# V loaded on all partitions, batch 0's q scaled at its cast, loads in another order, the low-rank product in one burst, and new priorities

## The chip, the cores and the metric

The kernel runs on one core of one Trainium2 chip. The metric is device time in microseconds (us) from one launch of the whole kernel; lower is better. The profile names the core's engines PE (TensorE), DVE (VectorE), ACT (ScalarE), POOL (GpSimd) and SP (SyncE, which here only issues DMAs). 16 DMA engines move data; their transfers are issued from SP's queue and from POOL's.

## What is computed

Four batches, each of 8 heads, 768 positions and 64 numbers per head. First a recurrent attention with a decay for each head, then a mixer: a low-rank product along the positions (U is 768x32, V is 32x768), added to x, and a two-layer perceptron along the 512 channels with 2048 hidden units.

```python
# attention, per batch and head
state = gamma * state + outer(k[t], v[t])
y[t] = scale * q[t] @ state
# mixer, x = y with heads side by side: (768, 512) per batch
h = xt @ U @ V                      # xt is x transposed
u = x + h.transpose(0, 2, 1)
ch = np.maximum(u @ w_ch1, 0.0) @ w_ch2
return u + ch
```

The kernel computes the recurrence in blocks: within a block as a masked product of q and k with v, between blocks over a state. The decay is split into a factor gamma^t on the side of q and gamma^-t on the side of k.

## The kernel before

**The planner.** The kernel doesn't issue its instructions in the order of the code. Each step is handed to `Plan.add` with a cost for each engine that may run it (letters PE, A for ACT, D for DVE, P for POOL, S for SP's DMA queue, Q for POOL's), what it reads and writes, a due time `at`, and sometimes an earliest time `hold`. `Plan.schedule` places them one by one: of the steps whose predecessors are placed it takes the one that can start first, and among equals the one with the smaller `at`. A step with several engines goes to the one where it would end first. The resulting order per engine is then written out and is fixed on the chip; the planned times and `hold` only decide that order, while on the chip semaphores decide when an instruction runs. Each engine works through its own list in order. The numbers of the dictionary `X` shift the due times; they have no other use, except `sp`, the distance of two batches, by which the due times of batch b start at `T[b] = 21 + sp*b`.

**Batch 0.** Loads of batch 0 are issued from SP in the order of `ORDER`, which is sorted by the entries `ok0`, `oq0` and so on of `X`: k0, q1, q2, q0, k1, V, v0, k2, v2, v1, k3, q3, U, v3. A digit names a pair of heads. `GATE`, the load before the last that is neither U nor V, is q3: the loads of w1 on POOL's queue wait for it to land, and everything that POOL loads later is in one chain behind them (`load_cast` writes the key "in turn").

`pair(c, ...)` computes one pair of heads: k is scaled with `gv` (`scale`, a product of two inputs), q is cast to bf16 (`cast`, a copy), v is cast; k and q are transposed by PE and evicted to `kT` and `qT`; `score` multiplies them in two pieces of 512 and 256 positions, each followed by a DVE product with a mask into `a`; `states` forms the states between blocks, evicted to `ns`; `query` and `intra` add both parts into one bank; `xout` scales this with `gqn` (gamma^t and the factor 1/8) on DVE into `x`. Then `low0(c)` does the low-rank part for these 128 channels (product with `Ub`, eviction to `pcs`, product with `V4`) and gives the transposed u, which the first layer reads.

Where the planner sees PE idle before 21.5 us of its time, `fill` puts in matmuls that nobody reads (`M<-gT` in the profile).

**V.** V is loaded as 32 rows of 768 numbers on 32 partitions (`Vin`, in the memory of T4), cast by ACT to `V4[:RK]`, copied to four groups of 32 partitions by a matmul with `rep` (four identities side by side, written by four ACT copies), and evicted in two pieces.

**Batches 1 to 3.** k, q and v are loaded in chunks of 128 positions; k and q (in batch 1 only k) are transposed by DMAs that SP issues (`t<-kb`, `t<-qb`), two chunks share one `score` step, then mask, state and `mixes`. `proj` makes the low-rank product with U of a whole batch into the bank Y, in two steps of four and of two blocks of x; `expand` multiplies with V and adds to x. `turn_u` transposes the sums by DMA (`uT<-x`) for the next MLP. `mlp` runs the two layers, the second with seven products instead of eight per block, which needs sums of g (`sums`) and of w2 (`w2_sums`, the tiles T).

## Time and profile before

| | |
|---|---|
| median of 3 runs without profile | 221.57 us (221.29 to 221.57) |
| the profiled execution | 224.22 us, of which the span from first to last instruction is 222.5 us |
| granted PE clock, mean | 1.000 |
| HBM read, written | 27.46 MB, 6.29 MB |
| matmuls of the first layer, M<-uT,w1b | 493, 85.6 us |
| last DVE eviction | 218.68 us, for 0.79 us |

The page of the profile lists the busy time of each engine, then the costliest groups of instructions. A group is a line of the kernel, an engine and an operation with its tiles, written out<-in. Many operations go through helpers and so share a line, L294 for nearly all matmuls; the tile names tell them apart. The timeline gives start, length, engine, line and tiles of runs of instructions; "x6" is six of them and a bracket names what ended the idle time ahead of it. The views by window cut the span into stretches. Times are from the start of the span.

### The profile page before, as it was taken

The page shows a single profiled execution, that of the slowest core. Times are in us where ns is not written, and L with a number is a line of the kernel's source. Part 1 is how long each engine was busy: PE and PEld are TensorE (multiplying, and loading weights), DVE is VectorE, ACT ScalarE, POOL GpSimd, SP SyncE. Part 2 cuts the span into 40 slices and gives each one's busy share as a digit, 9 for nine tenths or more (in the row PEclk, how much of TensorE's full clock was granted, in tenths as well). Part 3 has the DMA queues.
Part 4 walks back from the last instruction along what each step waited for, and adds up shares of the span by engine and source line. Part 5 has one row for each costly group of instructions (what it writes and reads, how often), then busy time and mean ns, then how long its engine had stood idle before and what let it go on. Part 6 is the DMA issues. An engine that isn't in the chain of part 4 may idle for free.

```text
span 222.5 us, 5665 instructions
## 1 busy us (share of the span) xinstructions
PE 211.5 (95%) x2321; PEld 151.8 (68%) x2334; DVE 143.7 (65%) x294; ACT 94.3 (42%) x182; POOL 101.7 (46%) x145
## 2 busy tenths in 40 slices
...
GB/s 164 308 311 124 154 204 210 209 176 213 190 91 239 142 160 195 219 138 150 163 110 195 192 198 292 99 0 3 3 93 144 97 97 0 0 3 0 97 94 94
DMA packets 84618, 30.98 MB, mean 139 GB/s; under 512 B 69328, under 2 KB 82384, under 8 KB 84592
## 3 DMA queue, kind: packets, MB, share of 16 engines
...
q8 instruction: 18, 0.29, 0.6%
...
HBM read 27.46 MB, written 6.29 MB: 152 GB/s over the span
## 4 chain that ended last, share of the span: by engine, by line
PE 68%; DVE 11%; DMA 10%; SPq 5%; issue 2%; ACT 1%; POOL 1%; DVEq 0%; POOLq 0%
PE M L294 58%; PE RR L294 7%; SPq L323 5%; DMA t<-kb 4%; DMA uT<-x 3%; DVE S L291 3%; DMA S<-in_q_dram 3%; DVE x L836 3%; PE Y L294 3%; DVE T L291 2%; DVE w2b L291 1%; DVE gT L291 1%; PE RR L298 1%; POOL t L291 1%; DVE o L1012 1%
## 5 line engine op out<-in xcount | busy, mean ns | idle before, releaser
L294 PE MATMUL M<-uT,w1b 128*128 128x256 bf16 (+1 forms) x493 | 85.6, 324 | 1.7 <-DMA uT<-x 1.0
L902 ACT ACTIVATE gT<-M 128x512 bf16<-128x512 f32 x93 | 55.0, 597 | 39.9 <-PE M L294 39.5
L294 PEld LDWEIGHTS <-w1b 128*128 128x128 bf16 x512 | 47.9, 98 | 31.1 <-DMA uT<-x 1.3
L294 PEld LDWEIGHTS <-gT 128*128 128x128 bf16 x423 | 40.8, 99 | 12.2 <-issue 3.9
L291 POOL TENSOR_TENSOR t<-s,x 128x256 f32<-128x256 f32 x36 | 23.1, 669 | 54.0 <-DVE S L291 38.7
L294 PEld LDWEIGHTS <-S 128*128 128x128 bf16 x288 | 27.6, 98 | 3.9 <-issue 0.5
L291 POOL TENSOR_TENSOR vb<-in,gkn 128x512 bf16<-128x512 f32 x18 | 18.8, 1048 | 24.2 <-DVE S L291 14.0
L287 ACT ACTIVATE s<-M 128x256 f32<-128x256 f32 x12 | 4.6, 383 | 51.4 <-PE M L294 51.4
L294 PE MATMUL M<-w2b,gT 128*128 128x256 bf16 x192 | 26.4, 273 | 0.0
L291 DVE TENSOR_TENSOR S<-gT 128x512 bf16<-128x512 bf16 x24 | 10.9, 456 | 23.4 <-ACT gT L902 23.4
L294 PE MATMUL M<-w2b,S 128*128 128x256 bf16 x192 | 26.1, 273 | 0.0
L294 PE MATMUL M<-T,gT 128*128 128x256 bf16 x192 | 25.2, 273 | 0.3 <-DVE r L1012 0.2
L759 DVE TENSOR_TENSOR a<-RR,mask 128x1024 bf16<-128x1024 f32 x18 | 21.6, 1218 | 2.3 <-PE RR L294 2.1
L332 POOL DMA_DIRECT2D kb<-in_k_dram x18 | 16.6, 920 | 4.6 <-PE M L294 4.0
L1012 DVE TENSOR_TENSOR r<-M,t 128x256 f32<-128x256 f32 x24 | 10.0, 422 | 11.5 <-POOL t L291 10.7
L836 DVE TENSOR_TENSOR x<-RR,x 128x512 bf16<-128x512 f32 x24 | 15.4, 682 | 2.7 <-PE RR L294 2.7
L1054 POOL DMA_DIRECT2D out_dram<-o x18 | 10.4, 581 | 11.3 <-DVE o L1012 11.3
L798 DVE TENSOR_TENSOR x<-RR,gqn 128x512 bf16<-128x512 f32 x18 | 12.3, 686 | 3.7 <-PE RR L294 3.7
L294 PEld LDWEIGHTS <-t 64*128 64x128 bf16 (+2 forms) x304 | 10.4, 98 | 6.1 <-issue 2.6
L1012 DVE TENSOR_TENSOR o<-M,r 128x256 f32<-128x256 f32 x24 | 10.1, 421 | 5.8 <-PE M L294 5.8
L287 ACT ACTIVATE ns<-Y 64x256 bf16<-64x256 f32 x28 | 10.5, 376 | 7.3 <-PE Y L294 6.1
L294 PE MATMUL M<-T,S 128*128 128x256 bf16 x96 | 12.6, 273 | 0.3 <-DVE T L291 0.3
...
## 6 DMA issues: line engine op xcount, KB each, us to landing
...
```

Of the source, the lines that this page charges most:

```text
L287: return nc.scalar.activation(dst, src, AF.Copy)
L291: return (nc.vector if e == "D" else nc.gpsimd).tensor_tensor(dst, a, b, op=op)
L294: nc.tensor.matmul(out_, lhsT, rhs, start=start, stop=stop, skip_group_check=True)
L298: nc.tensor.transpose(out_, in_, ident)
L323: ins = nc.sync.dma_start(out=dst, in_=src)
L332: ins = nc.gpsimd.dma_start(out=dst, in_=src)
L759: add({"D": cD(2 * DM)}, lambda e, a=a, lo=lo: nc.vector.tensor_tensor(a[:, :2 * DM].rearrange("p (n t) -> p n t", t=P), RR[lo // 2].rearr ...
L798: add({"D": cD(DM)}, lambda e, n=n, bank=bank: nc.vector.tensor_tensor(v8(xs[b % 2][:, n]), v8(bank), g8(gqn, n), op=ALU.mult), [bk, "gqn" ...
L836: add({"D": cD(512)}, lambda e, xj=xj, src=src: nc.vector.tensor_tensor(xj, src, xj, op=ALU.add), [f"RR{c}" for c in cc] + kk, kk + [("u", ...
L902: nc.scalar.activation(dst, src, AF.Relu)
L1012: add({"D": cD(HD)}, lambda e: nc.vector.tensor_tensor(dst, bankof(bank)[:, :HD], src, op=op), [bank] + rd, wr, at - X["dv"])
L1054: lambda e: (nc.sync if last else nc.gpsimd).dma_start(out=dst, in_=src), rd, [("out", b, at)], at,
```

## The change

Six things change.

1. V is loaded as 128 partitions of 192 numbers (partition 4r+z has quarter z of row r). A cast of 192 columns makes `Vb`; four selection matrices `sel`, made by four DVE comparisons of an iota `at4` on POOL with the partition number, each pick one quarter and copy it to four groups of 32 rows, in four matmuls of 192 columns; one eviction of 768 columns follows. `rep` is gone.
2. In batch 0 q is no longer copied to bf16 but multiplied with `gq` (gamma^t and 1/8, in the layout of q) by DVE or POOL, as the planner chooses; `xout` becomes a plain copy from the bank, on ACT or DVE. `gqn` is still used in batches 1 to 3 and made later. The k scaling of pairs 2 and 3 may go to DVE too.
3. Loads of batch 0: q1, k0, q0, q2, V, k1, v0, k2, v1, k3, v2, q3, U, v3. The gate is q3 as before.
4. `proj` is one step of six blocks.
5. The filler counts have other factors, and the first filler step is held to 2.3 us.
6. All other numbers of `X` are new, new ones are added that shift steps of `pair` and `low0`, and two planned costs of DMAs differ (packet lengths, the tail of a transpose).

```diff
 ALU = mybir.AluOpType
 
 
-X = dict(ok0=-5.67, oq0=1.84, ok1=1.9, oq1=-0.6, ov0=3.14, ok2=5.26, oq2=1.45,
-         ok3=15.06, oV=2.44, oq3=17.18, ov1=13.19, ov2=6.5, ov3=18.48, oU=18.06, lq=17.99,
-         tr=0.24, tq=10.94, ex=-12.82, rl=-2.43, su=-4.19, e0=10.6, h0=4.72, w2=13.24,
-         sp=49.61, s1=21.14, pl=7.44, dv=11.91, cs=-1.39, cm=-10.37, cz=-3.97, l01=18.56,
-         l11=8.4, lh1=7.26, lv1=-0.63, c01=16.51, c11=6.16, pr1=46.27, tu1=48.21, td1=7.82,
-         cd1=2.53, vd1=-4.64, l02=-11.92, l12=14.31, lh2=-6.66, lv2=-24.37, c02=8.2, c12=10.8,
-         pr2=24.03, tu2=46.43, td2=-2.58, cd2=-1.75, vd2=-9.06, l03=-9.78, l13=11.82,
-         lh3=-18.87, lv3=-4.29, c03=-2.28, c13=9.08, pr3=21.72, tu3=34.68, td3=5.36,
-         cd3=-10.86, vd3=2.96)
+X = dict(ok0=1, oq0=2, ok1=5, oq1=0, ov0=6, ok2=7, oq2=3, ok3=9, oV=4, oq3=11, ov1=8,
+         ov2=10, ov3=13, oU=12, lq=-45.23, tr=-14.91, tq=-38.01, ex=7.83, rl=-14.32, su=18.99,
+         e0=6.44, h0=5.37, w2=-3.71, sp=46.89, s1=48.11, pl=32.09, dv=17.7, cs=-53.8,
+         cm=-25.93, cz=13.57, l01=-35.68, l11=36.86, lh1=11.83, lv1=2.13, c01=39.94, c11=-6.13,
+         pr1=23.15, tu1=51.34, td1=66.28, cd1=-25.8, vd1=-20.06, l02=-6.29, l12=10.42, lh2=0.5,
+         lv2=-29.02, c02=-23.8, c12=1.28, pr2=10.89, tu2=25.84, td2=1.3, cd2=10.29, vd2=31.92,
+         l03=5.32, l13=13.9, lh3=-10.93, lv3=-39.66, c03=-25.14, c13=2.38, pr3=30.22, tu3=18.6,
+         td3=-54.16, cd3=-30.22, vd3=-22.97, ka0=42.09, ka1=-5.31, ka2=-11.97, ka3=6.36,
+         qa0=27.76, qa1=-35.86, qa2=-44.9, qa3=-88.92, va0=6.17, va1=7.23, va2=-25.67,
+         va3=38.79, sa0=22.39, sa1=-10.15, sa2=11.68, sa3=16.82, st0=0.17, st1=15.58,
+         st2=-6.01, st3=24.5, mx0=-8.83, mx1=27.0, mx2=-20.81, mx3=-39.06, lo0=-6.27,
+         lo1=34.38, lo2=1.06, lo3=-1.13)
 
 
 def Xb(n, b):
...
             if op.eng == "PE":
                 gap = op.start - last - 0.12
                 if fill and op.start < until and gap > 0.1:
-                    fill(int(gap * (1.25 if last < 13 else 1.0) / (0.44 if last < 4 else 0.218)))
+                    fill(int(gap / (0.36 if last < 4 else 0.2)))
                 last = op.free
             ins = op.fn(op.eng)
             if op.eng == "D" and "D" in op.lock:
...
     gv = sb.tile([P, NC, 2, NB, 2], fp32, name="gv")
     gqn = sb.tile([P, NCK, H], fp32, name="gqn")
     gkn = sb.tile([P, NCK, H], fp32, name="gkn")
+    gq = sb.tile([P, H, NCK], fp32, name="gq")
     ns = sb.tile([P, 12, P], bf16, name="ns")
 
     def ring(n, shape, dtype, name):
...
             lambda e: both(e, dst, src, g, ALU.mult), rd, wr, at, lock="DP")
 
     def packet(size):
-        return {128: 0.014, 256: 0.0195, 512: 0.0265}.get(size, 0.0055 + size / 27000)
+        return {128: 0.0135, 256: 0.0195, 512: 0.027, 1536: 0.065}.get(
+            size, 0.0055 + size / 27000)
 
     def load(dst, src, nd, size, wr, at, hold=0.0, rd=(), tail=1.0, held=None):
         def f(e):
...
     add({"D": 0.22}, lambda e: nc.vector.tensor_scalar(
         mask, jmat, srange[:, 0:1], None, op0=ALU.is_ge), rd=["jmat"], wr=["mask"],
         at=late + 6, hold=late + 6)
+    ramp(gq, [NCK, H, 1], [[0, H], [1, NCK]], NCK,
+         lgt[:, :, None].to_broadcast([P, H, NCK]), 1.0, "gq", late)
     for t, sign, key in ((gqn, 1.0, "gqn"), (gkn, -1.0, "gkn")):
         ramp(t, [NCK, H, 1], [[P, NCK], [0, H]], 1,
-             lgt[:, None, :].to_broadcast([P, NCK, H]), sign, key,
-             late if sign > 0 else 25.0)
+             lgt[:, None, :].to_broadcast([P, NCK, H]), sign, key, 25.0)
 
 
     def xk(b, nn, cc):
...
                  [(key, y) for y in ((0, 1) if g is None else (g,))] + ["turn"], at + 0.01 * z, hold,
                  tail=0.8 if (nm, c, z) == ("k", 0, 0) else 1.2, held=held)
 
+    KE, QE = ("D", "D", "PD", "PD"), ("PD", "PD", "PD", "PD")
+
     def pair(c, at, atq, atv, between):
 
         last = c == NC - 1
+        at, atq, atv = at + Xb("ka", c), atq + Xb("qa", c), atv + Xb("va", c)
+        ats, mat = atq + Xb("sa", c), max(atv + 2.6, atq + 4.5) + Xb("mx", c)
         (kin, kk), (qin, qk), (vin, vk) = (gets.pop((nm, 0, c)) for nm in "kqv")
         (kb, kbk), (qb, qbk), (vb, vbk), (kT, kTk), (qT, qTk) = (
             (t[:, :S], key) for t, key in (r() for r in (
...
             scale(blocks_of(kb, g), heads(kin, g),
                   gk[:, g[0]:g[0] + len(g)].to_broadcast([P, len(g), 6, D]), w,
                   [(kk, i) for i in g] + ["gv"], [(kbk, i) for i in g],
-                  at + 0.1 * g[0], eng="D" if c < 2 else "P")
-        cast(blocks_of(qb, (0, 1)), heads(qin, (0, 1)), S, both2(qk), both2(qbk), atq,
-             eng="PA")
+                  at + 0.1 * g[0], eng=KE[c])
+        scale(blocks_of(qb, (0, 1)), heads(qin, (0, 1)),
+              gq[:, 2 * c:2 * c + 2, :, None].to_broadcast([P, 2, NCK, D]), S,
+              both2(qk) + ["gq"], both2(qbk), atq, eng=QE[c])
         if last:
             vv = [t[:, :S].rearrange("p (i n x) -> p i n x", i=2, n=NB) for t in (vb, vin)]
             cast(vv[0][:, :, :2], vv[1][:, :, :2], 512, [(vk, 0)], [(vbk, 0)], atv,
...
         for bs in ((0, 1), (2,)):
             w = 256 * len(bs)
             add({"PE": 0.115 * len(bs) + (0.06 if last and bs[0] else 0)}, score(bs),
-                [kTk] + both2(qTk), keys, atq + 2.2 + 0.5 * bs[0], ("ss", "ss"))
+                [kTk] + both2(qTk), keys, ats + 2.2 + 0.5 * bs[0], ("ss", "ss"))
             held = []
 
             def masks(e, bs=bs, w=w, held=held):
...
                     .to_broadcast([P, 2, len(bs), 256]), op=ALU.mult))
 
             add({"D": cD(2 * w)}, masks, keys + ["mask2"], blocks(ak, bs),
-                atq + 2.4 + 0.5 * bs[0])
+                ats + 2.4 + 0.5 * bs[0])
 
             def copy_cross(e, held=held):
                 after(copy(e, cross[:64], RR[0][:64, :, 256:]), held[0])
 
             if last and bs[0]:
                 add({"A": cA(512)}, copy_cross, keys + blocks(ak, bs) + ["cross0"], ["cross", ("T", 0)],
-                    atq + 3.6)
+                    ats + 3.6)
 
         def state(parts, start):
             def f(e):
...
 
         whole = [(1, 0, P), (2, 0, P), (3, 0, P), (4, 0, P), (3, 1, P), (4, 1, P)]
         half = [(0, 0, 64), (2, 1, 64)] + ([] if last else [(4, 2, 64)])
-        sat = atv + (0.6 if last else 1.5)
+        sat = atv + (0.6 if last else 1.5) + Xb("st", c)
         vks = [(vbk, 0)] if last else both2(vbk)
 
         def states(e):
...
                        vb[:, ds(384 * i + P * 2 + D * j, D)], start=False)
 
         xv = xs[0].rearrange("p (b cc) f -> p cc b f", cc=2)
-        gx = gqn.rearrange("p (b cc) h -> p cc b h", cc=2)
-        mat = max(atv + 2.6, atq + 4.5)
 
         def both_(*fs):
             def f(e):
...
 
         def xout(cc, bs, bank, keys, at):
             n = len(bs)
-            add({"D": cD(P * n)}, lambda e: nc.vector.tensor_tensor(
-                xv[:, cc, ds(bs[0], n), ts(c, P)].rearrange("p b (i d) -> p b i d", d=D),
-                bank.rearrange("p (b i d) -> p b i d", i=2, d=D),
-                gx[:, cc, ds(bs[0], n), ds(2 * c, 2), None].to_broadcast([P, n, 2, D]),
-                op=ALU.mult), keys + ["gqn"], xk(0, [2 * b0 + cc for b0 in bs], [c]), at)
+            evac(xv[:, cc, ds(bs[0], n), ts(c, P)], bank.rearrange("p (b f) -> p b f", b=n),
+                 P * n, keys, xk(0, [2 * b0 + cc for b0 in bs], [c]), at)
 
         if not last:
             add({"PE": 0.28 + 0.36 + 0.093}, both_(query(range(1, NCK)), intra(range(NB))),
...
             for i, (src, sk) in enumerate(turned):
                 add({"S": 1.26}, lambda e, src=src, i=i, tr=tr: nc.sync.dma_start(
                     out=tr[:, i], in_=src[:, :DM], transpose=True), zz(sk),
-                    [(trk, i)], at - Xb("td", b), dma=(512, 0.0188, 0.7, 1.2))
+                    [(trk, i)], at - Xb("td", b), dma=(512, 0.0188, 0.7, 1.5))
             qT, qTk = [tr[:, 1, c] for c in ALLC], [(trk, 1)]
             if b == 1:
                 qT = [uTs[1][:, c, ts(n, P)] for c in ALLC]
...
                         mm(Y[ds(RK * c, RK), :P], Ub[:, j], xs[b % 2][:, j, ts(c, P)],
                            start=(j == 0), stop=(j == NCK - 1))
             return g
-        add({"PE": 0.25}, f(range(4)), xk(b, range(4), ALLC) + ["Ub"], ["Y"], at,
-            ("cn", "cn"), slack=sl)
-        add({"PE": 0.13}, f(range(4, 6)), xk(b, range(4, 6), ALLC) + ["Ub"], ["Y"],
-            at + 0.1, ("cn", "cn"), slack=sl)
+        add({"PE": 0.38}, f(ALLN), xk(b, ALLN, ALLC) + ["Ub"], ["Y"], at, ("cn", "cn"),
+            slack=sl)
         evac(pcs, Y[:, :P], P, ["Y"], ["pcs"], at + 0.3)
 
     def expand(b, j0, nj, at):
...
     def turn_u(b, j, at):
         add({"S": 1.26}, lambda e: nc.sync.dma_start(
             out=uTs[b % 2][:, :, ts(j, P)], in_=xs[b % 2][:, j], transpose=True),
-            [("u", b % 2, j, z) for z in range(2)], [("uT", b % 2, j)], at, dma=(512, 0.0188, 0.7, 1.2))
+            [("u", b % 2, j, z) for z in range(2)], [("uT", b % 2, j)], at,
+            dma=(512, 0.0188, 0.7, 1.5))
 
 
     W1 = [(0, 256), (256, 256), (512, 512), (1024, 512), (1536, 512)]
...
 
 
     zero = gT[:, 0, :512]
-    add({"PE": 0.43}, lambda e: mm(M[0], zero[:, :P], zero), rd=[("g", 0, 0)],
-        wr=["M0"], at=-10, mode=F)
+    add({"PE": 0.6}, lambda e: mm(M[0], zero[:, :P], zero), rd=[("g", 0, 0)],
+        wr=["M0"], at=-10, mode=F, hold=2.3)
 
     U0, FILL = 21.0, 21.5
     NAMES = [f"{n}{c}" for n in "kqv" for c in ALLC] + ["V", "U"]
...
     gate, GATE = [], [n for n in ORDER if n[0] not in "UV"][-2]
     Vin, Uin = T4.bitcast(fp32), T2.bitcast(fp32)
     Vin, Uin = (t_.rearrange("p a b -> p (a b)") for t_ in (Vin, Uin))
+    Vin = Vin[:, :S // 4]
     Uin = Uin[:, :NCK * RK].rearrange("p (j r) -> p j r", j=NCK)
     stage = [new_in() for _ in range(8)]
     for z, big in enumerate((S1, S2)):
...
         land[n] = t + 1.2
         at = -10 + land[n]
         if n == "V":
-            load(Vin[:RK, :S], moe_V, RK, 3072, ["Vin", "turn"], at, tail=1.2)
+            load(Vin, moe_V.rearrange("r (z x) -> (r z) x", z=4), P, S,
+                 ["Vin", "turn"], at, tail=1.2)
         elif n == "U":
             load(Uin, moe_U.rearrange("(j p) r -> p j r", p=P), S, 128,
                  ["Uin", "turn"], at, tail=1.2)
         else:
             load_pair(n[0], int(n[1]), at, stage.pop(0), held=gate if n == GATE else None)
 
-    rep = sb.tile([P, P], bf16, name="rep")
-
-    def repl(e):
+    QV = S // 4
+    sel = T3[:, ds(4, 2)].rearrange("p a (b m) -> p (a b) m", m=P)
+    Vb, at4 = T3[:, 6, :QV], tmp["r5"][:, :P]
+
+    def choose(e):
         for z in range(4):
-            copy(e, rep[:RK, ts(z, RK)], ident[:RK, :RK])
-    add({"A": 0.8}, repl, ["ident"], ["rep"], at=-2)
-
-    cast(V4[:RK], Vin[:RK, :S], S, ["Vin"], ["V1"], land["V"], eng="AP")
+            ins = nc.vector.tensor_scalar(sel[:, z], at4, srange[:, 0:1], float(-z),
+                                          op0=ALU.subtract, op1=ALU.is_equal)
+        return ins
+    add({"P": 0.3}, lambda e: iota(at4, [[0, 4], [4, RK]], 0), wr=["at4"], at=-2.5)
+    add({"D": 0.9}, choose, ["at4", "jmat"], ["sel"], at=4.5)
+    add({"A": cA(QV, True), "D": cD(QV)}, lambda e: copy(e, Vb, Vin), ["Vin"], ["Vb"],
+        land["V"])
 
     def rep_v(e):
-        mm(RR[1][:, 0], rep[:RK], V4[:RK, :512])
-        mm(RR[1][:, 1, :256], rep[:RK], V4[:RK, 512:])
-    add({"PE": 0.4}, rep_v, ["rep", "V1"], ["RR2", "RR3"], at=land["V"] + 1,
-        mode=("rn", "rn"))
-    evac(V4[:, :512], RR[1][:, 0], 512, ["RR2"], ["V1", "V4a"], land["V"] + 1.1, eng="AD")
-    evac(V4[:, 512:], RR[1][:, 1, :256], 256, ["RR3", "V4a"], ["V1", "V4"],
-         land["V"] + 1.2, eng="AD")
+        for z in range(4):
+            mm(RR[1][:, z // 2, ts(z % 2, QV)], sel[:, z], Vb)
+    add({"PE": 0.36}, rep_v, ["sel", "Vb"], ["RR2", "RR3"], at=land["V"] + 1, mode=F)
+    evac(V4.rearrange("p (z x) -> p z x", z=2), RR[1][:, :, :2 * QV], S, ["RR2"], ["V4"],
+         land["V"] + 1.1, eng="AD")
+
     def low0(c):
-        at = land[f"v{c}"] + (4.0 if c < 3 else 2.0)
+        at = land[f"v{c}"] + (4.0 if c < 3 else 2.0) + Xb("lo", c)
         x = xs[0]
         last = c == NC - 1
         r = ds(RK * c, RK)
```

## The prediction

> **What bounds the kernel now.** I read the page first, then busy time by stage, then the waits of the tensor engine, then the timeline of the stages that the change touches.
>
> ```profile
> span 222.5 us, 5665 instructions
> ...
> PE 211.5 (95%) x2321; PEld 151.8 (68%) x2334; DVE 143.7 (65%) x294; ACT 94.3 (42%) x182; POOL 101.7 (46%) x145
> ```
>
> From the page: PE is busy nearly throughout. That is no proof that nothing can be gained, because filler matmuls count as busy. So I cut the span at points where the timeline changes character.
>
> ```profile
> 1.33:21.40 20.07, 18.54 (x252) 10.21 (x255) 10.61 (x27) 11.61 (x23) 10.21 (x19) 1.00 0.89 247
> 21.40:32.00 10.60, 10.36 (x242) 7.32 (x242) 7.76 (x15) 6.04 (x14) 8.06 (x12) 1.00 1.15 170
> 32.00:46.00 14.00, 13.84 (x114) 6.95 (x113) 8.04 (x13) 9.94 (x17) 8.33 (x10) 1.00 1.38 208
> 46.00:58.00 12.00, 11.44 (x126) 8.72 (x126) 11.62 (x28) 7.71 (x16) 3.84 (x5) 1.00 1.45 194
> 58.00:72.00 14.00, 12.06 (x146) 10.13 (x144) 13.25 (x26) 3.38 (x9) 8.59 (x12) 1.00 1.33 168
> ...
> 122.00:140.00 18.00, 16.96 (x167) 12.55 (x167) 11.74 (x24) 4.76 (x11) 10.47 (x15) 1.00 1.75 216
> ...
> 200.00:222.50 22.50, 18.83 (x172) 16.49 (x169) 8.90 (x22) 1.84 (x5) 5.76 (x9) 1.00 0.19 71
> ```
>
> Columns: stretch, length, then busy time of PE, weight loads, DVE, ACT, POOL, the granted clock, the DMA share, GB/s. Three things are to be seen. From 21.4 us on PE has little air: what is left is 0.16 us in the third row, 0.56 in the fourth, 1.94 in the fifth, 1.04 in the sixth, 3.70 us together, and 3.67 us in the last row, which is the tail of last evictions and stores that nothing here touches. From 46 to 72 us DVE is busy 24.87 of 26 us, so there DVE limits beside PE. Before 21.4 us PE waits for the loads and fills in.
>
> ```profile
> PE M L294 <- DMA uT<-x: 1.0, 1, 1.0
> PE RR L294 <- DMA t<-kb: 0.9, 1, 0.9
> PE RR L294 <- DVE a L759: 0.6, 1, 0.6
> ```
>
> These are PE's three longest waits after 21 us: two transposing DMAs that landed late and a mask product. The start itself is paced by loads:
>
> ```profile
> 14.00:16.00 2.00, 1.69 (x42) 1.27 (x36) 2.00 (x3) 1.92 (x5) 1.44 (x1) 1.00 1.04 308
> 16.00:18.00 2.00, 1.91 (x66) 1.33 (x65) 1.48 (x2) 1.10 (x2) 1.64 (x2) 1.00 1.14 322
> 18.00:20.00 2.00, 1.58 (x45) 1.03 (x40) 1.83 (x4) 0.48 (x1) 0.87 (x2) 1.00 0.32 90
> 20.00:22.00 2.00, 1.47 (x51) 1.22 (x52) 1.04 (x2) 1.95 (x5) 2.00 (x3) 1.00 0.25 39
> ```
>
> Loads run at 308 to 322 GB/s up to 18 us and then fall off; the weights of the first MLP are held behind load q3. The bytes ahead of q3 are the same before and after the change (everything but U and v3), so I take this gate as fixed.
>
> **The change, part by part.** The profiled run's span is 222.5 us, and 1.7 us more lie around it (224.22 us in all). The median without a profile is 221.57. I work out differences in the span and put them on the median.
>
> *Load order and the scaled q.* The rows of the first pairs:
>
> ```profile
> 6.66 0.84 ACT L287 ACTIVATE qb<-in 128x768 bf16<-128x768 f32 x1 [2.21 <-DMA in<-in_q_dram]
> ...
> 8.23 0.82 POOL L288 CAST qb<-in 128x768 bf16<-128x768 f32 x1 [2.53 <-DMA in<-in_q_dram]
> ...
> 9.48 0.84 ACT L287 ACTIVATE qb<-in 128x768 bf16<-128x768 f32 x1 [1.29 <-DMA in<-in_q_dram]
> ...
> 10.38 0.51 PE L298 MATMUL M<-ident,qb 128*128 128x128 bf16 x6 [0.18 <-ACT qb L287]
> ...
> 10.73 1.24 PE L294 MATMUL M<-gT 128*128 128x512 bf16 x5
> 10.90 0.96 DVE L291 TENSOR_TENSOR kb<-in,gv 128x768 bf16<-128x768 f32 x1 [5.68 <-DMA in<-in_k_dram]
> 10.93 0.81 ACT L287 ACTIVATE t<-M 128x768 bf16<-128x768 bf16 x1 [0.60 <-PE M L298]
> ...
> 12.69 0.42 PE L294 MATMUL RR<-t,t 64*64 64x128 bf16 x16
> ...
> 13.96 1.47 POOL L291 TENSOR_TENSOR kb<-in,gv 128x768 bf16<-128x768 f32 x1 [0.46 <-DMA in<-in_k_dram]
> ```
>
> Before, q0 is the last of three q loads and is cast at 9.48; the first score runs at 12.69. After, the order is q1, k0, q0, q2, V, k1, v0, k2, v1, k3, v2, q3, U, v3, so q0 takes the arrival that q2 had, 8.23. k0 comes one load later, with q1 by 6.66, and its scaling, transposes and eviction (0.96+0.51+0.81) end by 9.0, still in time. q0's scaling costs 0.96 on DVE, by the k row of the same shape, where DVE is idle 5.68 us ahead of 10.90; its eviction takes 0.81. With 0.51 for its transposes that is 8.23+0.96+0.51+0.81 = 10.5 for the first score, about 2 us sooner. v1 ahead of v2 brings pair 1's states forward in the same sense.
>
> What does this pay? The stretch from 21.4 to 32 is 10.36 of 10.60 full of real PE work, so only work that moves ahead of it counts. Room for that: PE's idle time in the four rows from 14 to 22 us (0.31+0.09+0.42+0.53 = 1.35), and the 1.24 us of filler at 10.73. So the gain lies between nothing and 2.6 us. Against it stands q3:
>
> ```profile
> 19.52 0.84 ACT L287 ACTIVATE qb<-S 128x768 bf16<-128x768 f32 x1 [2.39 <-DMA S<-in_q_dram]
> ```
>
> q3 is the last q, its cast waits for the landing, and the score waits for it. Its scaling takes 0.96 on DVE or 1.47 on POOL instead of 0.84, so 0.12 to 0.63 us are lost there. Choosing POOL for the other three is covered by its waits for loads. The rows give POOL 1.47 against DVE 0.96, a factor of 1.5. [...]
>
> The scaling of the outputs goes from a DVE product to a plain copy on ACT or DVE:
>
> ```profile
> L642 DVE TENSOR_TENSOR x<-RR,gqn x8: 415/548/558, 18.1 to 29.5; 128x384 bf16<-128x384 f32 x6, 128x256 bf16<-128x256 f32 x2
> ```
>
> That is 6 x 0.55 + 2 x 0.42 = 4.1 us of DVE between 18 and 30, of which some goes to ACT, against about 3.8 us of q products, most of them before 15 us. DVE alternates masks and outputs in this stretch, so this helps to realise the earlier start more than it adds to it. I take for the start PE's idle 1.35 less 0.12 for q3: **-1.2 us**, bounds +0.6 and -2.6. The fillers are counted anew, 5 per us of planned gap instead of 5.7 up to 13 us; I price that inside these bounds.
>
> *V on 128 partitions.*
>
> ```profile
> 1.21 0.29 DVE L365 TENSOR_SCALAR ident<-jmat,srange 128x128 bf16<-128x128 f32 x1
> ...
> 11.63 0.83 ACT L287 ACTIVATE V<-T 32x768 bf16<-32x768 f32 x1
> ...
> 13.63 0.87 ACT L287 ACTIVATE V<-RR 128x512 bf16<-128x512 f32 x2 [0.36 <-PE RR L294]
> ...
> 20.26 0.35 ACT L287 ACTIVATE Ub<-T 128x192 bf16<-128x192 f32 x1
> ```
>
> ACT's cast of 768 columns becomes one of 192, 0.35 by ACT's 128x192 copy of U; two evictions of 0.87 become one of 0.81. Four selections on DVE (4 x 0.29 = 1.2) fall into DVE's idle time before 10.9. PE moves 768 columns as before. V4 is used only by the low-rank step, after U. So some 0.5 us of ACT go, at a place where ACT is not last: **0**, bounds +0.3 (the selections delay a k scaling by one of them) and -0.5. The load keeps its bytes.
>
> *Low-rank product in one burst.*
>
> ```profile
> 81.88 0.45 PE Y L294 x24
> ...
> 113.84 0.34 PE Y L294 x16
> ...
> 119.56 0.23 PE Y L294 x8
> ```
>
> Batch 1 already runs all 24 matmuls together (first row); batch 2 runs them in two pieces, 0.57 in sum. The eviction waits for both anyway, so nothing is late by joining them. **-0.1 us**, bounds 0 and -0.2.
>
> *Priorities.* The planner takes, on each engine, what can start first, and only ties go by priority. But MLP products and attention chunks are tied all the time, so nearly every due time counts. Batch length 49.61 becomes 46.89; the last sums of batch 2 (blocks 4 and 5 of x) were due at 70.6+24.0+4 = 98.6 and are due at 67.9+10.9+4 = 82.8, ahead of the products of the MLP before. The rows:
>
> ```profile
> 122.65 8.24 SPq L864 DMA_TRANSPOSE uT<-x  x6
> ...
> 134.20 0.39 PE L294 MATMUL M<-uT,w1b 128*128 128x512 bf16 x1 [0.99 <-DMA uT<-x]
> ```
>
> Batch 2's last transposes go out only by 130.9 and land at 134.2, while PE has run out of MLP work. Earlier sums put them out earlier, and this 1.0 us should go; that is the step I trust most. Queue order on POOL's DMAs is fixed by the program (one chain), so its loads don't move, whatever their new due times. For the 1.94 us from 58 to 72 I expect little: the late t<-kb depends on loads that don't move. Bounds: -3.7 (all idle time of the stages goes), and on the other side new waits of the size 0.9, one for each of the nine chunk scores but the one that has it, +7.2. I take **-0.9 us**, the one row less a tenth for the engine's change of work.
>
> Sum: -1.2 + 0 - 0.1 - 0.9 = -2.2 us; 221.57 - 2.2 = 219.4 us.
>
> **Rivals.**
>
> *Given back at DVE and w2 (near no change).*
>
> ```profile
> 55.29 0.88 POOL L332 DMA_DIRECT2D in<-in_v_dram  x1 [0.76 <-DMA w2b<-in_moe_w_ch_dram]
> ...
> 58.64 0.43 DVE L291 TENSOR_TENSOR T<-w2b,T 128x512 bf16<-128x512 bf16 x1
> 58.66 0.38 PE L294 MATMUL M<-T,S 128*128 128x256 bf16 x2 [0.29 <-DVE T L291]
> ```
>
> The last quarter of w2 lands about 55.2, fixed by the gate; its four sums (0.43 each, 1.7 together) make 57 the earliest end, and the product that needs them ran to 58.66. With DVE 24.87 of 26 us busy a start that is 1.2 us sooner only waits longer there. Then only the burst and a part of the uT wait remain: 221.57 - 0.1 - 0.2 = 221.3. For it: the DVE row. Against: 6 us of DVE idle from 32 to 46, and the due times of the w2 sums move ahead.
>
> *All of it works.* Start -2.6, burst -0.2, and the first three waits (1.0+0.9+0.6 = 2.5): -5.3, so 216.3. For it: the reasons above hold at once. Against: t<-kb hangs on loads that don't move.
>
> *New waits in PE's order (slower).* One mechanism: PE runs in order; chunk scores are put ahead of MLP products as soon as the plan believes their transposed k landed. The landings of the t transposes spread widely:
>
> ```profile
> DMA to landing us min/median/max: 3.0/5.4/10.6
> ```
>
> Each score that reaches PE's head too early costs some 0.9, as t<-kb did, with MLP products queued behind it. Two such waits eat the 1.3 us of start and burst; from there on the kernel is slower. With three and the uT wait as it was: -1.3 + 2.7 = +1.4, 223.0. For it: attention due times of batch 2 (first chunks 8.2 to -23.8) moved far ahead, and DMA shares of 1.3 to 1.75 from 32 to 140 make landings late. Against: only one such wait among nine scores now.
>
> **How the numbers follow.** Forecast 0.53, given back 0.15, all works 0.10, new waits 0.22. The forecast's own range goes from the start at its largest gain (219.4-1.4 = 218.0) to the start at its loss (219.4+1.8 = 221.2). The range reaches to the price of new waits, 223.0, and down to 217.0; a part of all works and the worse half of new waits lie outside, some 0.2. A measurement here can tell about 0.2%, 0.44 us. Faster: 0.50 of the forecast's share, 0.05 of given back, 0.10: 0.65. Same: 0.02 and 0.09: 0.11. Slower: 0.01, 0.01 and 0.22: 0.24.
>
> **What the profile after would show.** First score near 10.5 instead of 12.69; the first MLP matmuls of batch 0 in a row by about 30.8 instead of 32.04; the outputs' scaling gone from DVE; no uT<-x among PE's long waits and the six transposes out before 125; t<-kb still there once. It would be wrong if the first score is sooner and MLP still starts at 32 (PE order, not arrivals), if the idle time from 46 to 72 grows by what the start gained, or if PE shows three or more waits on t transposes.

## The result, and the profile after

The changed kernel took 224.83 us (median of 6 executions, 223.24 to 226.43) against 221.60 us of the kernel before on the same chip (6, 221.29 to 223.08): ratio **1.0122, 95% interval 1.0085 to 1.0159**, so about 2.7 us slower. A second set gave 225.26 against 222.46 us, ratio 1.0100 (1.0058 to 1.0141). The forecast of 219.4 us and its range up to 223.0 both missed; the sign is that of the rival "new waits in PE's order". A ratio leaves out executions over 1.5% longer than their kernel's fastest, for some kernels below nearly half of them, so a median over all executions, given where it tells more, can be up to 0.5% worse than the ratio says.

The page of the changed kernel, and its busy time by stage (columns as before):

```profile
span 221.6 us, 5665 instructions
...
PE 209.8 (95%) x2325; PEld 151.4 (68%) x2325; DVE 144.7 (65%) x300; ACT 95.2 (43%) x182; POOL 98.8 (45%) x143
```

```profile
21.40:32.00 10.60, 10.60 (x147) 6.22 (x147) 3.92 (x10) 7.45 (x18) 5.92 (x9) 1.00 1.20 184
...
58.00:72.00 14.00, 13.91 (x176) 12.21 (x175) 13.05 (x28) 2.92 (x8) 8.97 (x13) 1.00 0.88 155
...
97.00:122.00 25.00, 24.85 (x322) 21.16 (x320) 21.09 (x41) 9.48 (x21) 15.79 (x20) 1.00 1.41 153
122.00:140.00 18.00, 14.61 (x132) 9.69 (x129) 9.41 (x17) 4.56 (x9) 8.09 (x12) 1.00 1.59 173
140.00:160.00 20.00, 18.99 (x190) 13.76 (x191) 13.52 (x26) 10.91 (x19) 3.13 (x3) 1.00 0.40 60
```

The share of PE is the same 95%, and says nothing. The stages do: in this execution PE is idle from 122 to 160 us for 3.39 + 1.01 = 4.40 us. The waits of PE after 21 us in this execution name the cause:

```profile
PE RR L298 <- DMA t<-qb: 3.9, 2, 2.3
PE RR L302 <- DMA x<-in_q_dram: 1.2, 1, 1.2
PE Y L298 <- POOL vb L295: 0.5, 1, 0.5
PE RR L298 <- DVE a L765: 0.3, 1, 0.3
```

The waits for uT<-x and t<-kb are gone, that for the mask is halved. Two waits of a score for a transposed q have come, and they are 1.6 and 2.3 us long instead of 0.9.

To know what the start gained, the profile that the prediction read is not enough: that execution took 224.22 us, 2.6 us more than the median of 221.60. A second profile of the kernel before is of an execution of 221.89 us, and is the one compared with from here on.

> The kernel before once more, for the size of the start's gain. The profile of it that the prediction read had q3 cast at 19.52 us and the first layer of batch 0 in a row from 32.04. If the change's start is 3 to 4 us sooner because of the change, this profile shows q3 at 18.5 to 20 and the row at 31 to 33. If that profile was merely late (loads that came late in that one execution), q3 is at 17 to 18 here and the row at 28 to 30, and the start's true gain is 1 us or less. Time: 221.3 to 222.9 us.

Measured: 221.89 us, span 220.1; q3 is cast at 18.03, between the two ranges, and the row starts at 31.02, in the first. So that profile was late by 1.0 to 1.5 us, and the start still gains more than 1 us. Its timeline around the start, PE, ACT and POOL:

```profile
12.35 0.42 PE L294 MATMUL RR<-t,t 64*64 64x128 bf16 x16
...
18.03 0.84 ACT L287 ACTIVATE qb<-S 128x768 bf16<-128x768 f32 x1 [1.34 <-DMA S<-in_q_dram]
...
18.30 1.68 POOL L332 DMA_DIRECT2D w1b<-in_moe_w_ch_dram  x2 [0.65 <-DMA S<-in_q_dram]
...
31.02 4.28 PE L294 MATMUL M<-uT,w1b 128*128 128x512 bf16 x19
```

The changed kernel at the same places:

```profile
9.80 0.42 PE L298 MATMUL RR<-t,t 64*64 64x128 bf16 x16
...
17.00 0.96 DVE L295 TENSOR_TENSOR qb<-S,gq 128x768 bf16<-128x768 f32 x1 [0.34 <-DMA S<-in_q_dram]
...
17.27 3.93 POOL L337 DMA_DIRECT2D w1b<-in_moe_w_ch_dram  x5 [0.43 <-DMA S<-in_q_dram]
...
27.69 5.57 PE L298 MATMUL M<-uT,w1b 128*128 128x512 bf16 x25
```

The first score is 2.55 us sooner, q3 and the gate 1.0 us, the first layer in a row 3.33 us. In a second profile of the changed kernel they are at 10.49, 17.54, 17.82 and 28.52, so the gains are 1.9, 0.5, 0.5 and 2.5 us there. The prediction's profile, with the row at 32.04, would have put another 1.0 us on this.

Where the gain went is seen best at one point in each batch: the end of the last matmul of its first layer, read from PE's timeline (us).

| kernel, execution | batch 0 | batch 1 | batch 2 | batch 3 | span |
|---|---|---|---|---|---|
| before, 221.89 | 56.57 | 108.30 | 158.35 | 198.01 | 220.1 |
| changed, 223.40 | 53.78 | 107.03 | 158.93 | 199.58 | 221.6 |
| changed, second profile, 224.63 | 54.13 | 110.08 | 160.14 | 200.79 | 222.9 |
| lh2 4 us earlier (below), 220.04 | 53.94 | 107.07 | 155.57 | 196.21 | 218.3 |

The start is 2.4 to 2.8 us ahead at the end of batch 0's first layer. By the end of batch 2's it is gone: between the two points the changed kernel needs 105.2 and 106.0 us, the kernel before 101.8.

The points don't stand behind quite the same work. At the first, the kernel before has done one score of batch 1 that the changed kernel does just behind it (0.56 us), so the like-for-like gain of the start is 1.9 to 2.2 us. At the third, the kernel before has done most of batch 3's low-rank product, which the changed kernel does later (0.8 us of PE). Its rows, and the changed kernel's:

```profile
154.22 0.52 PE L294 MATMUL Y<-x,Ub 128*32 128x128 bf16 x24
...
157.30 1.05 PE L294 MATMUL M<-uT,w1b 128*128 128x256 bf16 x8
```

```profile
152.66 6.28 PE L298 MATMUL M<-uT,w1b 128*128 128x256 bf16 x56
...
162.36 0.52 PE L298 MATMUL Y<-x,Ub 128*32 128x128 bf16 x24
```

With both put right, the changed kernel loses 3.6 to 4.5 us between the points. The 0.8 us show again in the stretch up to batch 3's point, which takes 40.65 us against 39.66, and as long in the remedied kernel.

### The profile page after: what moved, and what is told of

Read it like the earlier page. It is cut to its first block, busy times and chain, and to the rows that moved or that the text cites. A ratio compares the mean times of both kernels' runs of the same rounds, so it can differ in the third digit from the quotient of the medians.

```text
span 221.6 us, 5665 instructions
## 1 busy us (share of the span) xinstructions
PE 209.8 (95%) x2325; PEld 151.4 (68%) x2325; DVE 144.7 (65%) x300; ACT 95.2 (43%) x182; POOL 98.8 (45%) x143
## 4 chain that ended last, share of the span: by engine, by line
PE 57%; DMA 19%; DVE 10%; SPq 7%; POOL 3%; issue 2%; ACT 1%; POOLq 0%; DVEq 0%
PE M L298 48%; DMA t<-qb 10%; DMA x<-in_q_dram 7%; PE RR L298 6%; SPq L328 5%; DMA S<-in_q_dram 3%; DVE S L295 3%; SPq L742 2%; DVE T L295 2%; POOL w1b L337 2%; PE Y L298 2%; DVE x L840 2%; DVE a L765 1%; POOL vb L295 1%; DVE gT L295 1%
## 5 line engine op out<-in xcount | busy, mean ns | idle before, releaser
L298 PE MATMUL M<-uT,w1b 128*128 128x256 bf16 (+1 forms) x504 | 87.3, 325 | 0.0
L298 PEld LDWEIGHTS <-gT 128*128 128x128 bf16 x412 | 39.7, 99 | 10.6 <-issue 3.7
L298 PE MATMUL M<-w2b,S 128*128 128x256 bf16 x192 | 26.6, 273 | 0.0
L291 ACT ACTIVATE ns<-Y 64x256 bf16<-64x256 f32 x26 | 9.8, 376 | 17.9 <-PE Y L298 13.6
## 6 DMA issues: line engine op xcount, KB each, us to landing
w1b<-in_moe_w_ch_dram POOLq DMA_DIRECT2D x3, 512.0 KB, 10.5
```

The lines of the kernel that those rows point to most:

```text
L291: return nc.scalar.activation(dst, src, AF.Copy)
L298: nc.tensor.matmul(out_, lhsT, rhs, start=start, stop=stop, skip_group_check=True)
```

## Why PE waits

A score of a pair of blocks needs four transposes (kb and qb of each block), issued from SP's queue. Rows of the changed kernel, SP and PE, and below them the time from issue to landing of the transposes issued at 124.14 and at 131.38 us, from the view of the DMAs narrowed to each:

```profile
99.60 0.94 PE L298 MATMUL RR<-t 64*128 64x128 bf16 x16
...
105.87 0.62 PE L298 MATMUL RR<-t 64*128 64x128 bf16 x16
...
114.55 7.97 SPq L868 DMA_TRANSPOSE uT<-x  x6
122.62 1.42 SPq L742 DMA_TRANSPOSE t<-kb  x1
124.14 1.41 SPq L742 DMA_TRANSPOSE t<-qb  x1
...
131.90 0.40 PE L298 MATMUL RR<-t 64*128 64x128 bf16 x8 [1.56 <-DMA t<-qb]
...
140.49 0.40 PE L298 MATMUL RR<-t 64*128 64x128 bf16 x8 [2.31 <-DMA t<-qb]
```

```profile
t<-qb SPq DMA_TRANSPOSE x1, 7.7
...
t<-qb SPq DMA_TRANSPOSE x1, 9.0
```

124.14 + 7.7 = 131.84 and 131.38 + 9.0 = 140.38: the two waits end 0.06 and 0.11 us after these landings. A score that isn't split and waits for nothing takes 0.62; the one at 99.60 took 0.94, since its last q landed at 95.03 + 5.0 = 100.03, after it had begun. So a small part of a wait hides in a long duration. The same places in the kernel before:

```profile
101.19 0.62 PE L294 MATMUL RR<-t 64*128 64x128 bf16 x16
...
112.89 2.10 SPq L736 DMA_TRANSPOSE t<-kb  x1
...
120.51 8.62 SPq L864 DMA_TRANSPOSE uT<-x  x6
...
128.60 0.62 PE L294 MATMUL RR<-t 64*128 64x128 bf16 x16
```

There batch 3's second block is transposed at 112.89, ahead of uT<-x; in the changed kernel at 122.62, behind it. All margins, worked out in this way (start of the score less the landing of its last transpose, us; below zero PE waits):

| | batch 2, 2nd pair | batch 2, 3rd pair | batch 3, 1st pair | batch 3, 2nd pair |
|---|---|---|---|---|
| before | +1.1 | +4.6 | +9.0 | +3.6 |
| changed | -0.4 | +0.6 | -1.9 | -2.6 |
| changed, second profile | -1.6 | -1.5 | -0.3 | -2.1 |
| lh2 4 us earlier | +0.1 | +2.6 | +1.0 | -0.3 |
| lh2 8 us earlier | +3.1 | +6.1 | +0.5 | -0.7 |

In the first execution the landings of batch 2 are no later than before (100.0 against 100.1, 105.3 against 106.5 us), and the scores come 1.6 and 5.2 us sooner. In batch 3 it is the other way round: the scores hardly moved (129.94 against 128.60, 137.78 against 139.16), and the landings come 12.2 and 4.8 us later. The changed kernel has next to no margin left: the first execution loses it mainly in batch 3, the second in both. The waits of PE in its second profile are in part put down to something else:

```profile
101.73 0.40 PE L298 MATMUL RR<-t 64*128 64x128 bf16 x8 [1.36 <-DVE a L765]
...
109.14 0.40 PE L298 MATMUL RR<-t 64*128 64x128 bf16 x8 [1.29 <-DVE a L765]
...
141.53 0.40 PE L298 MATMUL RR<-t 64*128 64x128 bf16 x8 [1.92 <-DMA t<-qb]
```

But the last transposes for these scores, issued at 97.00 and 103.19, took (view of the DMAs, narrowed to each)

```profile
t<-qb SPq DMA_TRANSPOSE x1, 4.6
...
t<-qb SPq DMA_TRANSPOSE x1, 5.8
```

so they landed at 101.60 and 108.99, 0.13 and 0.15 us ahead of the matmuls. The mask that ended in between belongs to the first half of the same score, and the second half, which writes another bank and stands ahead of that mask in the plan, has no need of it. I count all three as late transposes: 4.6 us in this execution, 3.9 in the first and the 0.3 that hides in its long score.

## The experiments

Two theories at first. **DUE**: the new priorities put scores where transposes have not landed, and the start is sound. Rival **START**: one of the three edits of the start loses time.

**Priorities put back, new start kept.** All entries of `X` but those of batch 0's start (`ok0` to `oU`, `ka0` to `lo3`) and the planned tail of a transpose are as before:

```diff
-                    [(trk, i)], at - Xb("td", b), dma=(512, 0.0188, 0.7, 1.5))
+                    [(trk, i)], at - Xb("td", b), dma=(512, 0.0188, 0.7, 1.2))
```

> The changed kernel with every due time that does not belong to batch 0's start (all of X but the load order and the new entries for pair and low0), and the planned tail of a transposing DMA, put back to the values of before. The profile of the changed kernel had the first long row of MLP matmuls at 27.69 us instead of 32.04. Theory DUE (the new due times of batches 1 to 3 make PE wait for transposed q and k, and so give back what the start gained): the row still starts at 27 to 28.5, and the time is 217 to 219.5 us. Rival STREAM (PE has caught up with the loads of batches 2 and 3, and any due times wait for them): the row starts at 27 to 28.5 and the time is 221.5 to 225.

Measured: 223.16 us, in STREAM's range and above DUE's; ratio 1.001 (0.9973 to 1.0047). So the loss goes with the priorities, but the old ones don't turn the start into time either. That kernel's longest waits of PE are 2.1 us for uT<-x and, in three parts, 1.1 for DVE's o.

**The counterpart**: the kernel before's start (copied q, old order, V on 32 partitions) under the other new priorities.

> The kernel before with only the due times outside batch 0's start, and the planned tail of a transpose, taken from the change; load order, q, V, fillers and proj as before. MLP row at about 32. DUE: the new due times lose 4 us or more on their own, so 224 to 228 us. STREAM: the start is as late as before, PE is not ahead of the loads, so 220 to 222.5 us.

Measured: 226.73 us, in DUE's range; ratio 1.0167 (1.0102 to 1.0233). The priorities alone cost about what the whole change does, or more; the intervals overlap. But the long wait of this kernel's profile is not for a transposed q or k:

```profile
102.38 0.38 PE L286 MATMUL Y<-vb,kb 128*128 128x128 bf16 x4 [2.01 <-POOL vb L283]
```

POOL's vb had itself waited for a v load that SP issued at 91.40 and that landed at 101.1. Late DMAs of SP's queue are the common part, and DUE in its words on scores holds for 0.8 us of waits here.

**One edit of the start undone at a time**, one execution each.

```diff
-X = dict(ok0=1, oq0=2, ok1=5, oq1=0, ov0=6, ok2=7, oq2=3, ok3=9, oV=4, oq3=11, ov1=8,
+X = dict(ok0=-5.67, oq0=1.84, ok1=1.9, oq1=-0.6, ov0=3.14, ok2=5.26, oq2=1.45,
...
-            load(Vin, moe_V.rearrange("r (z x) -> (r z) x", z=4), P, S,
-                 ["Vin", "turn"], at, tail=1.2)
+            load(Vin[:RK, :S], moe_V, RK, 3072, ["Vin", "turn"], at, tail=1.2)
...
-        scale(blocks_of(qb, (0, 1)), heads(qin, (0, 1)),
-              gq[:, 2 * c:2 * c + 2, :, None].to_broadcast([P, 2, NCK, D]), S,
-              both2(qk) + ["gq"], both2(qbk), atq, eng=QE[c])
+        cast(blocks_of(qb, (0, 1)), heads(qin, (0, 1)), S, both2(qk), both2(qbk), atq,
+             eng="PA")
```

> The changed kernel with the loads of batch 0 in the order of before (k0, q1, q2, q0, k1, V, v0, k2, v2, v1, k3, q3, U, v3); V on 128 partitions and q scaled as in the change. If the order is what brings the start forward, the first score is back at 12 to 13 us (9.80 in the changed kernel, 12.69 before) and the MLP row starts 1.5 us or more later than 27.69. If it is the arrival of q3 alone, the first score moves but the row stays within 0.7 us.

> The changed kernel with V on 32 partitions again (cast of 768 columns, rep matrix, two evictions). Read for the start alone: when q3 is cast or scaled (17.00 in the changed kernel, 19.52 before) and when the MLP row starts. If V's 32 long rows held the loads back, q3 is late again, 19 to 19.6, and the row starts 2 us or more later than 27.69. If V's layout does not matter to the loads, q3 stays at 17.0 and the row within 0.7 us of 27.69.

> The changed kernel with batch 0's q copied to bf16 again (on POOL or ACT) and its outputs scaled by gqn on DVE, as before; load order, V and due times as in the change. Read for the start: first score 9.80 and MLP row 27.69 in the changed kernel. If the scaling of q brings the start forward, the row starts 1 us or more later; if it is the order of loads alone, within 0.7 us of 27.69.

Measured: old order 224.42 us, V on 32 partitions 222.43, q copied 222.14; end of batch 0's first layer at 56.60, 55.24 and 55.68 us, against 53.78 (54.13 in the second profile); the row starts at 30.80, 30.81 and 30.14, against 27.69 (28.52). Each edit helps the start (by 2.8, 1.5 and 1.9 us, which overlap), none makes it later, as far as single executions tell; with V on 32 partitions the row is later though q3 is scaled at 17.09, and why is not shown. START is not settled by these: two of the three totals lie below every execution of the changed kernel (222.74 at least), though their start is worse. Being ahead is not what pays here; what the start is worth is measured at the end of this section. With the old order the plan puts q3 on POOL:

```profile
17.93 1.47 POOL L284 TENSOR_TENSOR qb<-S,gq 128x768 bf16<-128x768 f32 x1 [2.16 <-DMA S<-in_q_dram]
19.35 3.92 POOL L326 DMA_DIRECT2D w1b<-in_moe_w_ch_dram  x5
```

and w1, next on POOL, leaves 2.1 us later than in the changed kernel.

**The loads' earliest times.** I wrote that the numbers of `X`, `sp` apart, only shift due times; that is not so for `lh2` and `lh3`. They go into `hold`, the plan's earliest times for the first loads of batches 2 and 3. These times count from the batch before (`T[b-1]`): for batch 2 the change moves the time from 21 + 49.61 - 6.66 = 63.95 to 21 + 46.89 + 0.5 = 68.39 us of the plan, for batch 3 from 21 + 99.22 - 18.87 = 101.35 to 21 + 93.78 - 10.93 = 103.85, while PE comes sooner. HOLD: these loads set out too late. Rival STREAM: DMA could not deliver earlier anyway.

```diff
-         pr1=23.15, tu1=51.34, td1=66.28, cd1=-25.8, vd1=-20.06, l02=-6.29, l12=10.42, lh2=0.5,
+         pr1=23.15, tu1=51.34, td1=66.28, cd1=-25.8, vd1=-20.06, l02=-6.29, l12=10.42, lh2=-7.5,
...
-         l03=5.32, l13=13.9, lh3=-10.93, lv3=-39.66, c03=-25.14, c13=2.38, pr3=30.22, tu3=18.6,
+         l03=5.32, l13=13.9, lh3=-18.93, lv3=-39.66, c03=-25.14, c13=2.38, pr3=30.22, tu3=18.6,
```

> The changed kernel with two numbers of X moved by 8: lh2 0.5 to -7.5 and lh3 -10.93 to -18.93, the earliest planned times of the first loads of batches 2 and 3. In the changed kernel these loads went out at 72.1 and 100.2 us, as in the kernel before (72.4 and 101.1), though PE was 4 us ahead, and PE waited 3.9 us for transposed q. HOLD (the loads of batches 2 and 3 are let go too late for the earlier start): the first loads go out at 64 to 70 and 92 to 96 us, the waits for t<-qb after 90 us fall under 1 us together, and the time against before is a ratio of 0.980 to 0.995 instead of 1.012. STREAM (the DMA engines can't deliver sooner): the loads land as late as before, the waits stay at 3 us or more, ratio 1.005 to 1.015.

> The same kernel as g1_loads (the new kernel with only the two earliest times of the loads of batches 2 and 3, lh2 and lh3, put 8 us earlier each), for a tighter interval. Theory HOLD (the loads of batches 2 and 3 set out too late for a PE that is ahead, and that turns the start's gain into waits): ratio to before 0.984 to 0.993, again. Rival CHANCE (the four runs of g1_loads were scattered from 219.33 to 225.75, and the median was luck): 0.995 to 1.005.

Measured: 0.9884 (0.9788 to 0.9981), and again 0.9919 (0.9883 to 0.9956). STREAM falls. The first load of batch 2 left at 64.7 us, as HOLD said, that of batch 3 at 98.2 and not from 92 to 96. This kernel is not steady: five of the second set's eleven executions took 225.2 to 228.1 us and are not in the ratio; the median of all is 221.21 against 222.12 (0.996). The profile of one of the five, 225.68 us, has a wait of 4.05 us for t<-qb at 137.05. The same edit on the kernel with the old priorities (`lh2` and `lh3` 8 us earlier there):

> The kernel a_mid_old (start of the change, due times of before elsewhere, ratio 1.001) with the same two numbers moved by 8: lh2 -6.66 to -14.66, lh3 -18.87 to -26.87. HOLD: the start's 4 us come through, ratio 0.978 to 0.990. STREAM: 0.996 to 1.006 as without it.

Measured: 222.82, 226.16, 226.41 and 228.80 us, against a median of 222.66 of the kernel before. The spread leaves no ratio; not one of the four is near HOLD's 0.978 to 0.990. HOLD's remedy is shown under the new priorities only.

**SP's order alone**: batch 2's uT<-x held back in the plan, so that batch 3's early transposes go first, as in the kernel before. No load moves.

```diff
-            dma=(512, 0.0188, 0.7, 1.5))
+            dma=(512, 0.0188, 0.7, 1.5), hold=118.0 if b == 2 else 0.0)
```

> The changed kernel with only SP's order altered: the six transposes uT<-x of batch 2 are held to 118 us of the plan, so that on SP's queue they stand behind four transposes and two v loads of batch 3, as in the kernel before, instead of ahead of all but two. Loads on POOL as in the change. SPQ (the uT transposes, which wait for sums, block SP's queue and make t<-qb late): waits for t<-qb after 120 us under 1 us, ratio 0.990 to 1.003. HOLD: the loads are late all the same, and MLP of batch 2 now starts late too; ratio 1.005 to 1.020.

Measured: 0.9983 (0.9941 to 1.0025), in SPQ's range and below HOLD's; the median of all ten executions is 222.88 against 222.66 (1.001). In the profile, of the fastest of them (220.25 us), the waits for t<-qb come to 0.4 us. SP's order is a large part of the loss, not all of it: the start's gain doesn't come through.

**Which batch's loads?** One of the two entries at a time.

> The new kernel with lh3 alone 8 us earlier (-18.93 instead of -10.93): batch 3's loads of k and q may be issued from 95.9 us of the plan instead of 103.9, and with that the plan puts two of batch 3's transposes on SP's queue ahead of batch 2's uT<-x. Theory HOLD with batch 3 as the place of the loss: t<-qb among PE's waits falls from 3.9 to below 1 us, and the ratio to before is 0.985 to 0.996, as g1_loads. Rival HOLD with batch 2 as the place (lh2 is what g1_loads gained by): ratio 1.005 to 1.015, t<-qb stays above 2 us.

> The counterpart: lh2 alone 8 us earlier (-7.5 instead of 0.5), lh3 as in the change. The loads of batch 2 set out at about 64.7 us instead of 72.1, those of batch 3 at about 100 as in the change, and uT<-x stays ahead of batch 3's transposes on SP's queue. With batch 3 as the place of the loss: ratio 1.005 to 1.015 and t<-qb at 2 to 4 us in the stretch from 122 to 145. With batch 2 as the place: 0.985 to 0.996.

Measured: `lh3` alone **1.0201** (1.0151 to 1.0251), `lh2` alone **0.9917** (0.9887 to 0.9948). I had expected batch 3; it is batch 2. But `lh3` is no clean test of batch 3's loads: its first load left at 102.61 us, not sooner than in the changed kernel (100.23 and 101.70), by which time the second pair of batch 2 had already waited 1.97 us, where the changed kernel's second profile shows 1.36. What the edit moved are the next five loads, which left from 105 to 109 us instead of from 111 to 122, and SP's order: six of batch 3's transposes instead of two stand ahead of batch 2's uT<-x, which went out from 124.02 instead of 114.55 us. PE's longest wait comes just behind, 2.92 us for DVE, which waited for POOL; what links it to the new order is not shown:

```profile
126.18 0.42 DVE L1006 TENSOR_TENSOR r<-M,t 128x256 f32<-128x256 f32 x1 [3.41 <-POOL t L284]
```

```profile
126.66 1.01 PE L287 MATMUL M<-T,gT 128*128 128x256 bf16 x4 [2.92 <-DVE r L1006]
```

**Dose, and both remedies.** `lh2` 4 us and 12 us earlier; `lh2` 8 us earlier with SP's order put back.

> The dose between: lh2 4 us earlier (-3.5). In the plan the last loads of batch 2 leave by 82.8 us, as with 8 us earlier (82.4) and not as in the change (85.5). Theory HOLD in batch 2 (its last transposed q must land before PE comes to the score, and PE comes 3 us sooner than in the kernel before): already enough, 0.987 to 0.997, and no score between 90 and 110 us is split by a wait. Rival LUCK: 1.000 to 1.015, as the change itself.

> A dose: lh2 12 us earlier than in the change (-11.5). The first three loads of batch 2 may leave 57 to 59 us in the plan instead of 68.7, the rest about as with 8 us. Theory HOLD in batch 2 (its loads set out too late): as with 8 us, 0.985 to 0.997. Rival LUCK (each order of the plan has waits of its own): 1.000 to 1.015, with other waits of over 1 us on t or vb.

> Both remedies together: lh2 8 us earlier as in g10_lh2 (0.9917) and batch 2's uT<-x behind batch 3's early transposes on SP's queue as in g7_sp (0.9983). If they remove different waits: 0.982 to 0.990. If both remove the same two waits for t<-qb, which is what the traces say: 0.988 to 0.996, no better than lh2 alone. If the gain of lh2 is the luck of one order among many: anything from 0.99 to 1.01.

Measured: 4 us 0.9895 (0.9866 to 0.9924), 8 us 0.9917, 12 us 0.9900 (0.9861 to 0.9940), both remedies 0.9886 (0.9850 to 0.9923). By medians of all executions they are 0.990, 0.995, 0.995 and 0.990; with 4 us that counts two executions far outside (241.97 and 304.00 us). Three doses with three different orders of the plan agree within 0.3% by the ratio, within 0.5% by all executions, so this is not the luck of one order, and half the dose is enough. For both remedies together 0.9886 lies in the range for different waits and in that for the same ones, so it doesn't tell which. Rows of the kernel with 4 us, POOL's first load of batch 2 and PE's scores, and its longest waits:

```profile
68.72 0.94 POOL L337 DMA_DIRECT2D kb<-in_k_dram  x1
...
98.65 0.62 PE L298 MATMUL RR<-t 64*128 64x128 bf16 x16
...
105.03 0.62 PE L298 MATMUL RR<-t 64*128 64x128 bf16 x16
...
130.49 0.62 PE L298 MATMUL RR<-t 64*128 64x128 bf16 x16
```

```profile
PE RR L302 <- DMA x<-in_q_dram: 1.2, 1, 1.2
PE Y L298 <- POOL vb L295: 1.0, 1, 1.0
```

No score before 131 us is split, and no wait for t<-qb is left. These four versions beat both kernels; between them the intervals don't decide.

**What the start is worth**: the kernel before's start with the new priorities (1.0167 above), `lh2` 8 us earlier.

> The kernel before's start (its load order and its due times of batch 0, as in b_mid_new: 1.0167) under the change's other priorities, and lh2 8 us earlier. Theory HOLD in batch 2 with a start that is worth 2.8 us: the 2 us wait of b_mid_new near 98 to 100 us goes with the half-clock stretch behind it, and what is left is the remedied new kernel (0.9917) without its start, + 2.8 / 222 = 0.0126: 1.000 to 1.008. Rival (the start is worth nothing in the end, lh2 alone brings it below the kernel before): 0.988 to 0.996. Rival LUCK: as b_mid_new, 1.010 to 1.020.

Measured: 1.0073 (1.0031 to 1.0115), within HOLD's range. The remedy brings this one too about 1%, though the two intervals overlap a little. Against the changed kernel with the remedy (0.9895 to 0.9917) the start is worth 1.6 to 1.8%, 3.5 to 4 us with about 1 us of uncertainty, so the start as a whole loses nothing and START falls; the traces show 1.9 to 2.2 us at the start itself. One difference that they show is a wait of 1.2 us for t<-qb in this kernel, where the remedied ones have 0 to 0.4.

**The clock.** SPELL: a wait of some 2 us is followed by a stretch at half clock (0.64 and 0.50 in the two rows from 102 to 106 us of the kernel with `lh3` alone, in the last section), which is why many executions of the changed kernel have a mean clock of 0.992.

> The new kernel itself once more, for a second profile and more executions. Its first profile was of an execution with mean granted clock 0.998 (223.40 us), while five of its six executions had 0.990 to 0.992 and 223.24 to 226.43 us. Theory SPELL (a wait of PE of some 2 us or more is followed by about 3.4 us at half clock, which takes 0.5 x 3.4 / 222 = 0.008 from the mean clock and costs 1.7 us more): most executions again at 0.990 to 0.993, median 224 to 226, and if the profiled one is such, a stretch at a clock of 0.5 to 0.7 behind a wait for t<-qb between 128 and 145. Rival (the low clocks belong to the chip, not to this kernel): clocks as of the kernel before on this chip, 0.997 to 1.0, and a time of 222.5 to 223.5.

> The new kernel with ten more matmuls that nobody reads: five (128x512 each, about 0.22 us) in each of the two scores of batch 3 at which PE waited for t<-qb, between the half whose transposes have landed and the half that waits. The plan is untouched, the order on every engine too. They fill 1.1 us of each wait. Theory SPELL: the clocks of the executions rise to 0.997 to 1.0, and the median falls to 222.5 to 224.0, against 224 to 226 of the new kernel beside it, though PE has 2.2 us more to do. Rival WAITS ALONE (only the waits cost, their length is set by the landing of the transposes): the clocks stay as they are, and the time is the same within 0.3%, or longer by up to 2.2 us where the landing was earlier.

```diff
                 tr, lo, qT = got[n][4], got[n][8], got[n][9]
+                if b == 3 and n in (1, 3):
+                    for z in range(5):
+                        mm(RR[lo // 2][:, z % 2], w1b[:, z % 4, :P], w1b[:, z % 4, :512])
```

Measured: nine of the changed kernel's sixteen executions had a clock of 0.985 to 0.992, and one of the 18 of the kernel before beside the second set (seven of 85 over all sets that list it); with the fillers none of six (0.997 to 1.0), a seventh, of 428.32 us, being left out. In the second set it was four of ten, not most, as SPELL expected. With the fillers the median is 224.26 us, a little above SPELL's range, and the ratio 1.0069 (1.0035 to 1.0102), though PE has 2.2 us more to do, against 1.0100; the intervals overlap, so the clocks are shown and the time gained is not. The profiled second execution of the changed kernel had clock 1.0 and took 224.63 us by waits alone, so the half clock is an addition and not the cause of the loss.

## Why the prediction was wrong

**Load order and scaled q (-1.2 predicted).** Direction and place right, size too small: 1.9 to 2.2 us on the same work at the end of batch 0's first layer, V's part included. The first score came at 9.80 and 10.49, forecast 10.5. What was mis-sized is the cap: I counted PE's idle 1.35 us and kept the fillers for the bound only. But the gain is larger than that idle time, so the filled gaps were room too (28 fillers before 22 us instead of 37), and the gate, taken as fixed, moved by 0.5 to 1.0 us. q3 went to DVE in 0.96, as priced; POOL's 1.47 was seen with the old order. Both rows together give a factor of 1.53 between the engines, where the prediction had 1.5.

**V on 128 partitions (0).** The total doesn't tell (the one execution with the edit undone took 222.43 us); at the start the edit gave 1.1 to 1.5 us by that execution, above my bound of 0.5.

**Burst (-0.1).** The 24 products ran in one group of 0.45 us instead of 0.34 + 0.23. No run tried it alone.

**Priorities (-0.9).** This is the step that failed, in three places. First, the uT<-x wait did go, the six transposes were out at 122.5, "before 125" (125.5 in the second profile), and batch 2's first layer begins at 128.12 (131.16) instead of 134.20 (131.87 in the second profile of the kernel before). The reading was off in one thing: the wait at 134.20 ended with the fourth of the six, and the last landed at 135.6. But in going sooner the six passed batch 3's transposes on SP's queue, and then stood at its head waiting for DVE, with those behind them. SP's own waits in the changed kernel:

```profile
SPq L868 <- DVE o L1017: 5.8, 1, 5.8
```

The prediction named the transposes that move and not those they move past; with that order put back the loss is gone (0.9983). Second, "its loads don't move, whatever their new due times": right for the clock time (72.11 against 72.36 and 70.27 us for batch 2's first), wrong as a comfort. With PE ahead, a load that stays is late; and `lh2`, an earliest time that the change raised, does move it (to 68.72 when lowered by 4), which turns the loss into a gain (0.9895). Third, one late t<-kb in nine scores was taken as evidence against new waits, while the margins that decide, 1.1 to 9.0 us in the kernel before (2.2 to 7.9 in the profile that the prediction read), were not worked out, though SP's and PE's rows had them.

**The rival "new waits in PE's order".** It is what happened: scores reach PE's head before their transposes have landed, with the products queued behind them. Late were transposed q, not k, and not only because scores stand earlier: in batch 3 the landings came later. The sign "three or more waits on t transposes" came out in the second profile (three), not in the first (two). The price was off: 0.9 for each of three, where the two or three waits of an execution are 1.3 to 2.3 us each and come to 4.2 to 4.6; and the start that they eat is larger than I had it. The two errors partly cancel, and 223.0 fell 1.8 us short. "Given back at DVE and w2" did not happen: from 58 to 72 us PE is idle 0.09 us, against 1.94 before (0.69 in the second profile of the kernel before).

Open: why, for the same order on SP's queue from 103 us on, the transposes issued from 122 to 136 us took 7.7 to 9.0 us to land in the changed kernel and 4.6 to 7.0 with `lh2` 8 us earlier. The fourth load of batch 3 left at 111.47 instead of 101.30 us, but it had landed by 114.9, ahead of them, so it doesn't explain this by itself. So why the loads of batch 2 also cure batch 3's waits is not shown. Also open is what the new priorities cost beyond the late loads (1.0073 with the old start).
